# Score masks added by an identity product in the first three chunks of a sliding-window attention and rational feed-forward kernel, with a shorter weight decoding

## The chip, the core and the metric

The kernel runs on one core of a Trainium2 chip. The core has five engines that work side by side, each through its own list of instructions in order: TensorE (PE, with its weight loads shown apart as PEld), VectorE (DVE), ScalarE (ACT), GpSimd (POOL) and SyncE (SP), which here only issues transfers. An engine that waits holds up everything behind it in its list. The metric is the time of one execution on the device, in microseconds (us); lower is better.

## The reference

Attention with a window of 64 positions over 8 batches of 576 tokens, 8 heads of 64, and then a feed-forward layer whose activation is a quotient of two polynomials with given coefficients:

```python
scores = scale * np.matmul(q, k.transpose(0, 1, 3, 2))
mask = (rel >= 0) & (rel < window)
scores = np.where(mask, scores, -1000000000.0)
scores = scores - np.max(scores, axis=-1, keepdims=True)
attn = np.exp(scores)
attn = attn / (np.sum(attn, axis=-1, keepdims=True) + 1e-09)
x = np.matmul(attn, v)                  # to 4608 tokens x 512
h = x @ w_in                            # 512 x 2048
P = a[0] + a[1] * h + a[2] * h2 + a[3] * h3
Q = 1.0 + np.abs(b[0]) * np.abs(h) + np.abs(b[1]) * h2
out = (P / (Q + 1e-6)) @ w_out          # 2048 x 512
```

The two weight matrices reach the kernel as 64-bit floating-point numbers, seen as pairs of 32-bit words.

## The kernel before

**Chunks, units and steps.** The 4608 tokens are cut into 12 chunks of 384. For each chunk the attention is done in 4 units, one for every two heads. A unit computes scores (L182), masks and scales them (L188 or L192), takes the negated maximum of each row (L198), 6 exponentials with their sums (L201), divides (L203 to L205), transposes (L212, L214), multiplies by v (L223) and leaves the result as a high part and a low part, `xh` (L228) and `xl` (L229). Then each chunk takes 16 steps of the feed-forward layer, 192 in all. A step has a first product of 12 matmuls (L239, result `h` in PSUM, two buffers), a gate (L246 to L260: five ACT instructions, seven on DVE for the first 28 gates and six on DVE and one on POOL after that) that ends with the parts `gh` and `gl`, and a second product of 9 matmuls (L280) that adds to three PSUM tiles. The second product of a step is written three steps behind its first.

**Scores share one place.** Scores and transposes of all units use the same PSUM tile `ps_s`, of which there is one buffer (L175, L210). Whoever writes it next waits until the last reader of what stands there is done.

**Weights.** A weight tile (128 x 512 numbers, 512 KB) is loaded into one of two buffers `w_st` (L105, L107) and decoded into a high and a low part: ACT takes the absolute value of the high words (L113), DVE works through L114, L116, L117 and L118, ACT rounds the high part (L121), and DVE subtracts it (L122). L118 is the last to read the load's buffer, so it is what lets the load after next begin. There are 32 such tiles, 16 of `w_in` and 16 of `w_out`: 4 are asked for ahead of the first step, the others up to step 22.

**Order.** The code names, for each step, which loads, units and products belong to it; a scheduler then sets the order of every engine's list from that, so the lists interleave decoding, units and gates. While weights are decoded, DVE's list holds all three kinds of work. The division of a unit (L205) is on DVE in the first two chunks and on POOL from the third on.

Of the kernel before, what the change touches and what calls it, by code (L numbers as in the profile page):

```python
# [9 lines left out]
F32 = mybir.dt.float32  # L10
# [9 lines left out]
PR = TC // 2  # L20
# [5 lines left out]
NEG = -1.0e9  # L26
BIG = 3.0e38
# [4 lines left out]
def swa_rational_ffn(ctx: ExitStack, tc: tile.TileContext, qT, kT, v, w_in, w_out, a, b, out):  # L32
# [32 lines left out]
    mask = const.tile([P, NM, P], F32, name="mask")  # L65

    def make_mask():
        nc.gpsimd.memset(mask, BIG)
        for j in range(NM):
            for half in range(2):  # L70
                off = 0 if FIRST.get(j) == half else WIN
                r = mask[half * 64:half * 64 + 64, j, :]
# [5 lines left out]
                                        fill=NEG, base=WIN - 1 - off, channel_multiplier=-1)  # L78

# [11 lines left out]
    make_identity(nc, ident)  # L91

# [8 lines left out]
    def decode(src, hi, lo):  # L101
# [11 lines left out]
        nc.scalar.activation(cf, w.bitcast(F32)[:, :, 1], AF.Abs)  # L113
        nc.vector.tensor_scalar(out=cf, in0=cf, scalar1=2.0 ** -15, scalar2=None, op0=ALU.max)  # L114

        nc.vector.tensor_scalar(out=c, in0=c, scalar1=3, scalar2=0x3FFFFFF8, op0=ALU.logical_shift_left, op1=ALU.bitwise_and)  # L116
        nc.vector.scalar_tensor_tensor(out=c, in0=low, scalar=29, in1=c, op0=ALU.logical_shift_right, op1=ALU.bitwise_or)  # L117
        nc.vector.scalar_tensor_tensor(out=c, in0=high, scalar=0xC0000000, in1=c, op0=ALU.bitwise_and, op1=ALU.bitwise_or)  # L118
        if len(hi.shape) == 3:
            cf = cf.rearrange("p (c n) -> p c n", c=hi.shape[1])  # L120
        nc.scalar.copy(out=hi, in_=cf)  # L121
        nc.vector.tensor_tensor(out=lo, in0=cf, in1=hi.bitcast(F32), op=ALU.subtract)  # L122
# [49 lines left out]
    def unit_scores(c, hp):  # L172
        u = live[c, hp]

        ps = ps_a.tile([P, 2, 512], F32, name="ps_s", bufs=1)  # L175
        for p in range(PR):
            for z in range(2):
                for e in range(2):
# [4 lines left out]
                                     k[:, w:w + P], start=True, stop=True)  # L183
        sm = att.tile([P, 2, PR * P], F32, name="sm")
        m0 = u["m0"]
        for z in range(2):
            if m0 is None:
                nc.vector.scalar_tensor_tensor(out=sm[:, z, :].rearrange("p (r c) -> p r c", c=P),  # L188
                                               in0=ps[:, z, 0:PR * P].rearrange("p (r c) -> p r c", c=P), scalar=SCALE,
                                               in1=mask[:, 1:2, :].broadcast_to([P, PR, P]), op0=ALU.mult, op1=ALU.min)  # L190
            else:
                nc.vector.scalar_tensor_tensor(out=sm[:, z, :], in0=ps[:, z, 0:PR * P], scalar=SCALE,  # L192
                                               in1=mask[:, m0:m0 + PR, :].rearrange("p r c -> p (r c)"),
                                               op0=ALU.mult, op1=ALU.min)
# [194 lines left out]
```

## Time and profile before

| | us |
|---|---|
| median of 3 runs (1023.78 to 1029.62) | 1024.69 |
| the profiled execution's own time | 1025.14 |
| its span, first to last instruction | 1023.3 |
| PE busy | 953.1 (93%) |
| DVE busy | 850.3 (83%) |
| ACT busy | 725.8 (71%) |
| POOL busy | 233.7 (23%) |
| mean granted TensorE clock | 0.978 |

Two parts are to be told apart: a first one of some 200 us, in which weights are decoded, and the rest. A share over the whole span mixes them. In rows of the timeline the columns are start, duration, engine, line, operation, output<-input, shapes, count, and in brackets the engine's idle time before it with what ended that. Instructions of one engine overlap a little, so what one costs in a full queue is the distance from its start to the next start, not its duration.

### The profile page before, as it was taken

The page shows a single profiled execution, that of the slowest core. Times are in us where ns is not written, and L with a number is a line of the kernel's source. Part 1 is how long each engine was busy: PE and PEld are TensorE (multiplying, and loading weights), DVE is VectorE, ACT ScalarE, POOL GpSimd, SP SyncE. Part 2 cuts the span into 40 slices and gives each one's busy share as a digit, 9 for nine tenths or more (in the row PEclk, how much of TensorE's full clock was granted, in tenths as well). Part 3 has the DMA queues.
Part 4 walks back from the last instruction along what each step waited for, and adds up shares of the span by engine and source line. Part 5 has one row for each costly group of instructions (what it writes and reads, how often), then busy time and mean ns, then how long its engine had stood idle before and what let it go on. Part 6 is the DMA issues. An engine that isn't in the chain of part 4 may idle for free.

```text
span 1023.3 us, 18244 instructions
## 1 busy us (share of the span) xinstructions
PE 953.1 (93%) x6624; PEld 840.4 (82%) x6624; DVE 850.3 (83%) x1639; ACT 725.8 (71%) x1734; POOL 233.7 (23%) x231
## 2 busy tenths in 40 slices
PE   2677876899999999999999999999999999999997
PEld 2565755788898898898898898898898898888996
DVE  5999999998878878878878878878888888888785
ACT  4675765577767867867867867867867867866664
POOL 2000010002322322322322322322322322322221
PEclk9878989899999999999999999999999999999999
DMA  6634433111112112111112112111112112100000
GB/s 197 205 99 133 133 94 111 50 50 55 60 30 60 61 31 65 64 31 58 60 30 61 61 31 65 64 32 58 60 31 60 62 31 65 65 16 2 31 1 31
DMA packets 68537, 64.09 MB, mean 63 GB/s; under 512 B 4448, under 2 KB 61792, under 8 KB 68448
## 3 DMA queue, kind: packets, MB, share of 16 engines
q1 hardware_dynamic: 68448, 62.93, 19.8%
q8 instruction: 52, 0.85, 0.4%
q14 instruction: 37, 0.30, 0.1%
HBM read 53.48 MB, written 9.44 MB: 61 GB/s over the span
## 4 chain that ended last, share of the span: by engine, by line
PE 81%; DVE 11%; ACT 3%; DMA 3%; issue 1%; POOL 0%; SPq 0%; POOLq 0%; ACTq 0%; DVEq 0%
PE o L280 37%; PE h L239 35%; PE ps_x L223 3%; PE ps_s L182 3%; PE ps_s L212 3%; DMA w_st<-w_in 1%; DVE w_c L117 1%; DMA w_st<-w_out 1%; ACT sm L201 1%; DVE w_c L118 1%; DVE num L259 1%; DVE gh L257 1%; DVE u L258 1%; DVE num L249 1%; DVE num L250 1%
## 5 line engine op out<-in xcount | busy, mean ns | idle before, releaser
L239 PE MATMUL h<-xl,wi_h 128*128 128x384 f32 x768 | 264.9, 345 | 14.8 <-DVE num L250 8.6
L239 PE MATMUL h<-xh,wi_h 128*128 128x384 f32 x768 | 260.6, 339 | 0.0
L239 PE MATMUL h<-xh,wi_l 128*128 128x384 f32 x768 | 259.7, 338 | 0.0
L280 PE MATMUL o<-wo_h,gl 128*128 128x512 f32 x576 | 238.1, 413 | 22.3 <-DVE gl L260 22.3
L252 POOL TENSOR_TENSOR u<-u,ah 128x384 f32<-128x384 f32 x164 | 166.7, 1017 | 317.3 <-ACT u L248 278.7
L280 PE MATMUL o<-wo_h,gh 128*128 128x512 f32 x576 | 231.7, 402 | 0.0
L280 PE MATMUL o<-wo_l,gh 128*128 128x512 f32 x576 | 230.2, 400 | 0.0
L249 DVE TENSOR_TENSOR num<-num,h 128x384 f32<-128x384 f32 x192 | 106.1, 553 | 108.9 <-ACT num L247 108.7
L246 ACT ACTIVATE ah<-h 128x384 f32<-128x384 f32 x192 | 94.3, 491 | 108.1 <-PE h L239 83.3
L205 POOL TENSOR_TENSOR sm<-sm,rs 128x768 f32<-128x768 f32 x40 | 61.7, 1541 | 457.9 <-DVE rs L204 352.3
L201 ACT ACTIVATE sm<-sm,nmx 128x128 f32<-128x128 f32 x288 | 111.9, 390 | 76.4 <-DVE nmx L198 76.4
L239 PEld LDWEIGHTS h<-xl,wi_h 128*128 128x128 f32 x768 | 145.4, 189 | 23.3 <-DVE num L250 11.3
L280 PEld LDWEIGHTS o<-wo_h,gl 128*128 128x128 f32 x576 | 111.3, 193 | 51.3 <-DVE gl L260 24.6
L239 PEld LDWEIGHTS h<-xh,wi_h 128*128 128x128 f32 x768 | 145.5, 189 | 4.6
L239 PEld LDWEIGHTS h<-xh,wi_l 128*128 128x128 f32 x768 | 145.4, 189 | 0.0
L248 ACT ACTIVATE u<-ah,b_sb 128x384 f32<-128x384 f32 x192 | 135.4, 706 | 0.0
L280 PEld LDWEIGHTS o<-wo_h,gh 128*128 128x128 f32 x576 | 111.2, 193 | 26.1
L257 DVE SCALAR_TENSOR_TENSOR gh<-num,a_sb,ah 128x384 fp32r<-128x384 f32 x192 | 114.8, 615 | 17.6 <-ACT ah L256 16.9
L247 ACT ACTIVATE num<-h,a_sb 128x384 f32<-128x384 f32 x192 | 128.2, 668 | 0.0
L280 PEld LDWEIGHTS o<-wo_l,gh 128*128 128x128 f32 x576 | 111.8, 194 | 19.4
L250 DVE SCALAR_TENSOR_TENSOR num<-num,a_sb,h 128x384 f32<-128x384 f32 x192 | 117.9, 614 | 5.9
L259 DVE SCALAR_TENSOR_TENSOR num<-num,a_sb,u 128x384 f32<-128x384 f32 x192 | 115.8, 620 | 0.8
(45 smaller groups left out, 1090.3 us busy)
## 6 DMA issues: line engine op xcount, KB each, us to landing
out<-ob SPq DMA_DIRECT2D x33, 256.0 KB, 2.0
w_st<-w_in SPq DMA_DIRECT2D x16, 512.0 KB, 4.4
w_st<-w_out SPq DMA_DIRECT2D x16, 512.0 KB, 3.6
q<-qT SPq DMA_DIRECT2D x32, 192.0 KB, 3.3
vt<-v SPq DMA_DIRECT2D x16, 384.0 KB, 3.4
vt<-v SPq DMA_DIRECT2D x16, 320.0 KB, 3.9
kt<-kT SPq DMA_DIRECT2D x16, 224.0 KB, 3.6
kt<-kT SPq DMA_DIRECT2D x16, 192.0 KB, 3.6
```

Of the source, the lines that this page charges most:

```text
L201: nc.scalar.activation(sm[:, j, :], sm[:, j, :], AF.Exp, bias=nmx[:, j:j + 1], accum_out=sums[:, j:j + 1])
L205: (nc.vector if c < 2 else nc.gpsimd).tensor_tensor(out=sm, in0=sm, in1=rs.unsqueeze(2).broadcast_to([P, NR, P]), op=ALU.mult)
L239: nc.tensor.matmul(h, w[:, cc, i * P:(i + 1) * P], x[c, cc], start=n == 0, stop=n == 3 * NCC - 1)
L246: nc.scalar.activation(ah, h, AF.Abs)
L247: nc.scalar.activation(num, h, AF.Identity, scale=a_sb[:, 3:4], bias=a_sb[:, 2:3])
L248: nc.scalar.activation(u, ah, AF.Identity, scale=b_sb[:, 1:2], bias=b_sb[:, 0:1])
L249: nc.vector.tensor_tensor(out=num, in0=num, in1=h, op=ALU.mult)
L250: nc.vector.scalar_tensor_tensor(out=num, in0=num, scalar=a_sb[:, 1:2], in1=h, op0=ALU.add, op1=ALU.mult)
L252: (nc.vector if n_gates[0] <= DEC else nc.gpsimd).tensor_tensor(out=u, in0=u, in1=ah, op=ALU.mult)
L257: nc.vector.scalar_tensor_tensor(out=gh, in0=num, scalar=a_sb[:, 0:1], in1=ah, op0=ALU.add, op1=ALU.mult)
L259: nc.vector.scalar_tensor_tensor(out=num, in0=num, scalar=a_sb[:, 0:1], in1=u, op0=ALU.add, op1=ALU.subtract)
L280: nc.tensor.matmul(acc[c][t], g[:, ts], w[:, i, :], start=first and n == 0, stop=last and n == 2)
```

## The change

**Masks.** The mask tile held 3e38 where a score is kept and -1e9 where not, and DVE took the smaller of mask and scaled score. It now holds 0 and -1e30 and is added. It is built in a buffer that the units use later (`sm`), and an ACT copy rounds it to the type of TensorE's single-pass products. For the first three chunks (`PEM = 3`, 12 units of 48) TensorE adds it: two products of an identity with the mask (L188 of the change) open the accumulation in `ps_s`, and the score products add to that. DVE then takes the row maximum from PSUM (L202) and scales the six numbers of each row (L203), and the exponentials read PSUM with the scale built in (L213). The two mask instructions of DVE (L188 or L192 before) are gone in these units. From the fourth chunk on DVE still scales and adds the mask, two instructions a unit as before.

**Decoding.** ACT's absolute value now also scales by 2^-111, which makes the lower bound (L114) and the clearing of the top bits in the shift (L116) needless; DVE's L114 is gone, and the factor 2^-8 that puts the exponent right again is built into the ACT copy and the DVE subtraction at the end (L125, L126).

```diff
--- before.py
+++ after.py
@@ -23,8 +23,8 @@
 LAG = 3
 W_AT = 0, 1, 2, 3
 WLEAD = len(W_AT)
-NEG = -1.0e9
-BIG = 3.0e38
+NEG = -1.0e30
+PEM = 3
 QADD = 1.0 + 1e-6
 
 
@@ -62,20 +62,22 @@
     FIRST = {0: 0, 3: 1}
     MASKS = {0: 0, 3: 2}
     NM = 5
-    mask = const.tile([P, NM, P], F32, name="mask")
+    mask = const.tile([P, NM, P], F32R, name="mask")
 
     def make_mask():
-        nc.gpsimd.memset(mask, BIG)
+        raw = att.tile([P, 2 * PR, P], F32, name="sm")
+        nc.gpsimd.memset(raw[:, 0:NM, :], 0.0)
         for j in range(NM):
             for half in range(2):
                 off = 0 if FIRST.get(j) == half else WIN
-                r = mask[half * 64:half * 64 + 64, j, :]
+                r = raw[half * 64:half * 64 + 64, j, :]
 
                 nc.gpsimd.affine_select(out=r, in_=r, pattern=[[-1, P]], compare_op=ALU.is_ge,
                                         fill=NEG, base=off, channel_multiplier=1)
 
                 nc.gpsimd.affine_select(out=r, in_=r, pattern=[[1, P]], compare_op=ALU.is_ge,
                                         fill=NEG, base=WIN - 1 - off, channel_multiplier=-1)
+        nc.scalar.copy(out=mask, in_=raw[:, 0:NM, :])
 
     a_sb = const.tile([P, 4], F32, name="a_sb")
     b_raw = const.tile([P, 2], F32, name="b_raw")
@@ -89,6 +91,8 @@
     make_mask()
     ident = const.tile([P, P], F32, name="ident")
     make_identity(nc, ident)
+    ident_r = const.tile([P, P], F32R, name="ident_r")
+    nc.scalar.copy(out=ident_r, in_=ident)
 
 
     wi_h = const.tile([P, NCC, DFF], F32R, name="wi_h")
@@ -110,16 +114,16 @@
         cf = c.bitcast(F32)
 
 
-        nc.scalar.activation(cf, w.bitcast(F32)[:, :, 1], AF.Abs)
-        nc.vector.tensor_scalar(out=cf, in0=cf, scalar1=2.0 ** -15, scalar2=None, op0=ALU.max)
-
-        nc.vector.tensor_scalar(out=c, in0=c, scalar1=3, scalar2=0x3FFFFFF8, op0=ALU.logical_shift_left, op1=ALU.bitwise_and)
+
+        nc.scalar.activation(cf, w.bitcast(F32)[:, :, 1], AF.Abs, scale=2.0 ** -111)
+
+        nc.vector.tensor_scalar(out=c, in0=c, scalar1=3, scalar2=None, op0=ALU.logical_shift_left)
         nc.vector.scalar_tensor_tensor(out=c, in0=low, scalar=29, in1=c, op0=ALU.logical_shift_right, op1=ALU.bitwise_or)
-        nc.vector.scalar_tensor_tensor(out=c, in0=high, scalar=0xC0000000, in1=c, op0=ALU.bitwise_and, op1=ALU.bitwise_or)
+        nc.vector.scalar_tensor_tensor(out=c, in0=high, scalar=0x80000000, in1=c, op0=ALU.bitwise_and, op1=ALU.bitwise_or)
         if len(hi.shape) == 3:
             cf = cf.rearrange("p (c n) -> p c n", c=hi.shape[1])
-        nc.scalar.copy(out=hi, in_=cf)
-        nc.vector.tensor_tensor(out=lo, in0=cf, in1=hi.bitcast(F32), op=ALU.subtract)
+        nc.scalar.activation(hi, cf, AF.Copy, scale=2.0 ** -8)
+        nc.vector.scalar_tensor_tensor(out=lo, in0=cf, scalar=2.0 ** -8, in1=hi.bitcast(F32), op0=ALU.mult, op1=ALU.subtract)
 
     def load_w_in(i):
         sl = slice(i * P, (i + 1) * P)
@@ -173,6 +177,15 @@
         u = live[c, hp]
 
         ps = ps_a.tile([P, 2, 512], F32, name="ps_s", bufs=1)
+        m0 = u["m0"]
+        on_pe = c < PEM
+        if m0 is None:
+            mm = mask[:, 1:2, :].broadcast_to([P, PR, P])
+        else:
+            mm = mask[:, m0:m0 + PR, :]
+        if on_pe:
+            for z in range(2):
+                nc.tensor.matmul(ps[:, z, 0:PR * P].rearrange("p (r c) -> p r c", c=P), ident_r, mm, start=True, stop=False)
         for p in range(PR):
             for z in range(2):
                 for e in range(2):
@@ -180,25 +193,27 @@
                     k = u["kt"][z * 64:z * 64 + 64].rearrange("p t s -> p (t s)")
                     w = u["kw"][j] * WIN
                     nc.tensor.matmul(ps[e * 64:e * 64 + 64, z, p * P:(p + 1) * P], u["q"][z * 64:z * 64 + 64, j, :],
-                                     k[:, w:w + P], start=True, stop=True)
-        sm = att.tile([P, 2, PR * P], F32, name="sm")
-        m0 = u["m0"]
-        for z in range(2):
-            if m0 is None:
-                nc.vector.scalar_tensor_tensor(out=sm[:, z, :].rearrange("p (r c) -> p r c", c=P),
-                                               in0=ps[:, z, 0:PR * P].rearrange("p (r c) -> p r c", c=P), scalar=SCALE,
-                                               in1=mask[:, 1:2, :].broadcast_to([P, PR, P]), op0=ALU.mult, op1=ALU.min)
-            else:
-                nc.vector.scalar_tensor_tensor(out=sm[:, z, :], in0=ps[:, z, 0:PR * P], scalar=SCALE,
-                                               in1=mask[:, m0:m0 + PR, :].rearrange("p r c -> p (r c)"),
-                                               op0=ALU.mult, op1=ALU.min)
-        sm = sm.rearrange("p z (r c) -> p (z r) c", c=P)
+                                     k[:, w:w + P], start=not on_pe, stop=not on_pe or p == PR - 1)
+        sm = att.tile([P, 2 * PR, P], F32, name="sm")
         NR = 2 * PR
         nmx = att.tile([P, NR], F32, name="nmx")
-        nc.vector.tensor_reduce(out=nmx, in_=sm, axis=AX.X, op=ALU.max, negate=True)
+        if on_pe:
+            pss = ps[:, :, 0:PR * P].rearrange("p z (r c) -> p z r c", c=P)
+            nc.vector.tensor_reduce(out=nmx.rearrange("p (z r) -> p z r", z=2), in_=pss, axis=AX.X, op=ALU.max, negate=True)
+            nc.vector.tensor_scalar(out=nmx, in0=nmx, scalar1=SCALE, scalar2=None, op0=ALU.mult)
+        else:
+            for z in range(2):
+                nc.vector.scalar_tensor_tensor(out=sm[:, z * PR:(z + 1) * PR, :],
+                                               in0=ps[:, z, 0:PR * P].rearrange("p (r c) -> p r c", c=P), scalar=SCALE,
+                                               in1=mm.bitcast(F32), op0=ALU.mult, op1=ALU.add)
+            nc.vector.tensor_reduce(out=nmx, in_=sm, axis=AX.X, op=ALU.max, negate=True)
         sums = att.tile([P, NR], F32, name="sums")
         for j in range(NR):
-            nc.scalar.activation(sm[:, j, :], sm[:, j, :], AF.Exp, bias=nmx[:, j:j + 1], accum_out=sums[:, j:j + 1])
+            if on_pe:
+                nc.scalar.activation(sm[:, j, :], ps[:, j // PR, (j % PR) * P:(j % PR + 1) * P], AF.Exp, scale=SCALE,
+                                     bias=nmx[:, j:j + 1], accum_out=sums[:, j:j + 1])
+            else:
+                nc.scalar.activation(sm[:, j, :], sm[:, j, :], AF.Exp, bias=nmx[:, j:j + 1], accum_out=sums[:, j:j + 1])
         rs = att.tile([P, NR], F32, name="rs")
         nc.vector.tensor_scalar(out=sums, in0=sums, scalar1=1e-9, scalar2=None, op0=ALU.add)
         nc.vector.reciprocal(out=rs, in_=sums)
```

**What the lists look like now.** The scheduler orders anew, so the lists differ from the first row on. First DVE at the start of the program: `w_c` is a weight tile in decoding, `nmx` the row maxima of a unit, `sums` and `rs` belong to its division. Before:

```order
L114 TENSOR_SCALAR w_c<-w_c 128x512
L192 SCALAR_TENSOR_TENSOR sm<-ps_s,mask 128x384 x2
L116 TENSOR_SCALAR w_c<-w_c 128x512
L198 TENSOR_REDUCE nmx<-sm 128x6
L117 SCALAR_TENSOR_TENSOR w_c<-w_st,w_c 128x512
L118 SCALAR_TENSOR_TENSOR w_c<-w_st,w_c 128x512
```

and of the change, at the same place:

```order
L120 TENSOR_SCALAR w_c<-w_c 128x512
L121 SCALAR_TENSOR_TENSOR w_c<-w_st,w_c 128x512
L122 SCALAR_TENSOR_TENSOR w_c<-w_st,w_c 128x512
L126 SCALAR_TENSOR_TENSOR wi_l<-w_c,wi_h 128x4x128
L120 TENSOR_SCALAR w_c<-w_c 128x512
L121 SCALAR_TENSOR_TENSOR w_c<-w_st,w_c 128x512
L122 SCALAR_TENSOR_TENSOR w_c<-w_st,w_c 128x512
L120 TENSOR_SCALAR w_c<-w_c 128x512
L202 TENSOR_REDUCE nmx<-ps_s 128x6
L121 SCALAR_TENSOR_TENSOR w_c<-w_st,w_c 128x512
L126 SCALAR_TENSOR_TENSOR wi_l<-w_c,wi_h 128x4x128
L203 TENSOR_SCALAR nmx<-nmx 128x6
```

The first unit's row maximum stood behind the beginning of the first decoding; it now stands behind two whole shift-and-merge passes and the first instruction of the third tile (L120), and its scaling (L203) behind two more decoding instructions.

Then PE at the start of the program, where `ps_s` passes from unit to unit. Before:

```order
L182 MATMUL ps_s<-kt,q 64x128 x24
L212 MATMUL ps_s<-ident,sm 128x128 x6
L182 MATMUL ps_s<-kt,q 64x128 x12
L223 MATMUL ps_x<-pT,vt 64x64 x12
L212 MATMUL ps_s<-ident,sm 128x128 x6
```

and of the change:

```order
L188 MATMUL ps_s<-mask,ident_r 128x384 x2
L195 MATMUL ps_s<-kt,q 64x128 x12
L188 MATMUL ps_s<-mask,ident_r 128x384 x2
L195 MATMUL ps_s<-kt,q 64x128 x12
L227 MATMUL ps_s<-ident,sm 128x128 x6
L188 MATMUL ps_s<-mask,ident_r 128x384 x2
L195 MATMUL ps_s<-kt,q 64x128 x12
L238 MATMUL ps_x<-pT,vt 64x64 x12
L227 MATMUL ps_s<-ident,sm 128x128 x6
```

The sequence of units, transposes (L212, now L227) and products with v (L223, now L238) is the same, with two mask products ahead of each unit's scores.

Last, DVE at the end of the decoding, where `wo_l` is the low part of the last `w_out` tile. Before, the rows around it (it is the last L122 of the list) are

```order
L118 SCALAR_TENSOR_TENSOR w_c<-w_st,w_c 128x512
L257 SCALAR_TENSOR_TENSOR gh<-num,a_sb,ah 128x384
L258 SCALAR_TENSOR_TENSOR u<-u,gh 128x384
L257 SCALAR_TENSOR_TENSOR gh<-num,a_sb,ah 128x384
L122 TENSOR_TENSOR wo_l<-w_c,wo_h 128x512
```

and of the change

```order
L202 TENSOR_REDUCE nmx<-ps_s 128x6
L265 SCALAR_TENSOR_TENSOR num<-num,a_sb,h 128x384
L126 SCALAR_TENSOR_TENSOR wo_l<-w_c,wo_h 128x512
L122 SCALAR_TENSOR_TENSOR w_c<-w_st,w_c 128x512
L275 TENSOR_TENSOR gl<-num,ah 128x384
L203 TENSOR_SCALAR nmx<-nmx 128x6
L272 SCALAR_TENSOR_TENSOR gh<-num,a_sb,ah 128x384
L126 SCALAR_TENSOR_TENSOR wo_l<-w_c,wo_h 128x512
```

Counted through DVE's list, before the last tile's subtraction follows 18 finished gates (18 `gl`, 20 gates begun), and of the change 11 finished gates (12 begun). Ahead of the first `gl` the list of before holds 11 whole decodings, and that of the change 18: the decoding is moved ahead, to between the units of the first chunk.

## The prediction

> **What bounds the kernel now.** First the page's slices of the span, 25.6 us each, tenths of busy time (9 means 90% or more):
>
> ```profile
> PE   2677876899999999999999999999999999999997
> DVE  5999999998878878878878878878888888888785
> ```
>
> DVE is full in slices 2 to 9 and PE from slice 9 on, so the kernel has two parts. The windows, cut at the end of the first gate (65.6) and where PE stops idling (202.2), give for each stretch its length and the busy us (instruction counts) of PE, PEld, DVE, ACT, POOL, then granted clock, DMA share, GB/s:
>
> ```profile
> 0.00:40.00 40.00, 16.66 (x173) 13.46 (x174) 29.40 (x59) 21.47 (x68) 6.88 (x27) 0.94 0.66 199
> 40.00:65.60 25.60, 16.22 (x171) 13.71 (x169) 24.27 (x50) 18.39 (x50) 0.00 (x0) 0.82 0.54 160
> 65.60:202.20 136.60, 104.77 (x630) 86.55 (x630) 132.21 (x264) 87.19 (x204) 7.22 (x3) 0.90 0.33 103
> 202.20:1007.60 805.40, 805.35 (x5617) 719.25 (x5618) 658.79 (x1260) 593.42 (x1406) 217.94 (x200) 1.00 0.15 46
> ```
>
> From 202.2 PE is busy 805.35 of 805.40 us: whatever PE work is left there takes its full time. Before, DVE is the bound (132.21 of 136.60). Who waited for whom in the first 205 us (us, times, longest) says how:
>
> ```profile
> PE o L280 <- DVE gl L260: 20.3, 9, 4.0
> ```
>
> PE's second products wait for the gates' last DVE instruction. So the end is the time at which DVE lets PE run full, plus PE's work then left, plus a tail.
>
> **What a DVE instruction costs.** In a full queue, start to next start, from DVE's timeline:
>
> ```profile
> 96.19 0.42 DVE L116 TENSOR_SCALAR w_c<-w_c 128x512 uint32<-128x512 uint32 x1
> 96.53 0.62 DVE L259 SCALAR_TENSOR_TENSOR num<-num,a_sb,u 128x384 f32<-128x384 f32 x1
> 97.05 0.69 DVE L117 SCALAR_TENSOR_TENSOR w_c<-w_st,w_c 128x512 uint32<-128x512 uint32 x1
> 97.66 1.02 DVE L192 SCALAR_TENSOR_TENSOR sm<-ps_s,mask 128x384 f32<-128x384 f32 x2
> 98.59 0.55 DVE L260 TENSOR_TENSOR gl<-num,ah 128x384 fp32r<-128x384 f32 x1
> 99.05 0.69 DVE L117 SCALAR_TENSOR_TENSOR w_c<-w_st,w_c 128x512 uint32<-128x512 uint32 x1
> ...
> 100.72 0.95 DVE L198 TENSOR_REDUCE nmx<-sm 128x6 f32<-128x768 f32 x1
> 101.59 0.68 DVE L118 SCALAR_TENSOR_TENSOR w_c<-w_st,w_c 128x512 uint32<-128x512 uint32 x1
> ...
> 105.70 0.18 DVE L203 TENSOR_SCALAR sums<-sums 128x6 f32<-128x6 f32 x1
> 105.77 0.69 DVE L122 TENSOR_TENSOR wi_l<-w_c,wi_h 128x512 fp32r<-128x512 f32 x1
> ...
> 107.47 0.42 DVE L114 TENSOR_SCALAR w_c<-w_c 128x512 f32<-128x512 f32 x1
> 107.81 0.61 DVE L257 SCALAR_TENSOR_TENSOR gh<-num,a_sb,ah 128x384 fp32r<-128x384 f32 x1
> ```
>
> L114 and L116 cost 0.34 each; L117, L118 and L122 0.60; a unit's two mask instructions 0.93; the row maximum 0.87, and the division, as long, the same; a 128x6 instruction some 0.09. A gate's seven cost 0.47 or 0.53 each (L260, L259), together 3.47. So the change removes 32 x 0.34 = 10.9 us (L114) and 12 x 0.93 = 11.2 us (masks), adds 12 x 0.09 = 1.1 us (L203), and DVE has **21.0 us** less to do, all in the part that it bounds.
>
> Edits with one answer: the shift loses its second operation but passes the same 128x512 (kept at 0.34); L122 becomes a three-operand form like L117's, 0.60 as before; ACT's scales ride on instructions that exist. The row maximum now reads PSUM: no row has a reduction from PSUM, but two of 128x384, one reading PSUM (L249), one not (L260), agree:
>
> ```profile
> L249 DVE TENSOR_TENSOR num<-num,h 128x384 f32<-128x384 f32 x192 | 106.1, 553 | 108.9 <-ACT num L247 108.7
> L260 DVE TENSOR_TENSOR gl<-num,ah 128x384 fp32r<-128x384 f32 x192 | 103.0, 553 | 1.6
> ```
>
> So I take 0.87 again; at worst twice that, +10.4 us for twelve, at best the two-a-time pace of L116 (512 in 0.34), -4. [...]
>
> On PE the 24 mask products are like first products (12 in 2.09, below), 0.175 each and 4.2 us in all. Those of the first units lie in PE's idle time; the last two units' lie where PE is full and are counted below. The mask's ACT copy comes while ACT would wait for a load.
>
> **Where the reorder puts it.** By the order's rows the lists differ at once, so I walk the change's lists by hand, with durations from these rows (the chain's columns: start, us, what):
>
> ```profile
> 7.73 0.67 ACT w_c L113
> ...
> 10.03 0.96 DVE nmx L198
> 11.01 2.42 ACT sm L201 x12
> ...
> 26.96 4.34 DMA w_st<-w_in
> ...
> 39.87 3.50 DMA w_st<-w_out
> ```
>
> and compare with these of before:
>
> ```profile
> 17.31 1.51 PE L212 MATMUL ps_s<-ident,sm 128*128 128x128 f32 x6 [5.87 <-DVE sm L205]
> 28.00 0.55 DVE L229 TENSOR_TENSOR xl<-ps_x,xh 128x384 fp32r<-128x384 f32 x1
> 47.30 0.55 DVE L229 TENSOR_TENSOR xl<-ps_x,xh 128x384 fp32r<-128x384 f32 x1
> 51.89 1.01 DVE L249 TENSOR_TENSOR num<-num,h 128x384 f32<-128x384 f32 x2
> 65.08 1.01 DVE L260 TENSOR_TENSOR gl<-num,ah 128x384 fp32r<-128x384 f32 x2
> ```
>
> The first unit's maximum now stands behind the third tile's L120. The first decoding starts at 8.4, behind ACT's 7.73 + 0.67, and its three dependent DVE instructions free the buffer at 10.3; the third tile's load starts then, lands 4.4 later, and ACT takes 0.67: L120 at 15.4, the maximum at 15.8 (10.03 in the chain of before). L203 stands behind two more decoding instructions, so the exponentials run 18.0 to 20.4 and hold `ps_s`, which before was free once DVE had masked. Unit 2: maximum 24.8, exponentials 27.0 to 29.4; only then the first transposes, 29.5 against 17.31. The third maximum (34.8) has the eighth tile's L120 between it and its L203: load asked for at 33.1, landed 37.5, L120 at 38.2, exponentials 38.6 to 41.0. First `xl` 41.5 (28.00). Then exponentials of unit 4 from 50.1 to 52.5, transposes of units 3 and 4 at 52.6 and 54.9 (each waits for `ps_s`), the last `xl` 66.4 (47.30), first gate instruction 71.3 (51.89), first gate done **83.8** (65.6). Up to there DVE's list holds 57.9 us of work by the costs above, so it idles 25.9 us, against 65.6 - 51.9 = 13.7 before. The lead eats 12.2 of the 21.0 us, but it has done 18 decodings, not 11.
>
> From the first to the 12th `gl`, where the change's decoding ends, DVE's list holds 14 decodings (2.14 each), 11 gates, 4 maxima, 2 divisions, 4 `xl` and the small ones: 75.1 us. The 20th `gl` of before is
>
> ```profile
> 202.67 0.56 DVE L260 TENSOR_TENSOR gl<-num,ah 128x384 fp32r<-128x384 f32 x1
> ```
>
> and from the first to there the list of before held 129.4 us by the same costs and took 203.2 - 65.6 = 137.6, 1.064 of it. With that, 75.1 x 1.064 = 80 and the 12th `gl` comes at **163.8**.
>
> PE's two kinds of products, undisturbed, from the chain:
>
> ```profile
> 970.05 4.19 PE h L239 x24
> 974.24 4.14 PE o L280 x18
> ```
>
> 2.09 for a first product of 12 and 2.07 for a second of 9. From the 12th `gl` on DVE needs 28.1 us for the next 8 gates and PE 34, so PE is full from then on, 38 us sooner than at 202.2. But it has more left: by the order's count 15 first and 11 second products are done, where before it was 22 and 18. That is 7 x (2.09 + 2.07) = 29.1, one unit's scores and two units' transposes, 0.8 each (an estimate: half of the 1.51 of the transposes at 17.31, when PE ran at half its pace), and the last two units' masks 0.7: 32.3 us. Gain: 202.2 - 163.8 - 32.3 = 6.1 us.
>
> The tail of before:
>
> ```profile
> 1013.64 0.51 PE L280 MATMUL o<-wo_h,gl 128*128 128x512 f32 x1 [1.95 <-DVE gl L260]
> ```
>
> There four second products end the list: two run, PE waits 1.95 us for a gate, and two follow. Now one first product and three second ones end it, with one wait of about 2.9 for the last gate and half as much PE work behind it, which a lowered clock could stretch: within 1 us either way, taken as 0. So the span comes to 1023.3 - 6.1 = 1017.2, and the time to 1025.14 - 6.1 = **1019.0**, from the profiled execution's own time, which is 0.45 over the median of the runs and within their spread.
>
> **The rivals.**
>
> *The lead's holes close.* If loads land earlier than in the walk, or the waits fall elsewhere, DVE idles 13.7 as before: first gate 71.6, 12th 151.6, and the gain is 18.3: 1006.8. For it: loads wait only for buffers, DMA share 0.66. Against: the reorder's rows put the maxima behind loads whatever their speed. Chance 0.22.
>
> *The lead starves more.* The slow side: two buffers feed 16 decodings ahead of the first gate, and DVE's list now has little else. If a load takes 6.0 us instead of 3.5 to 4.4, some ten waits in the lead grow by 1.7: first gate at 101, 1036. It costs more than it gains from 0.6 us a load on. For it: in the first 40 us DMA already moves 199 GB/s; against: those loads landed in 4.34 and 3.50 there. Chance 0.12.
>
> *PE becomes late in the middle.* Exponentials now hold `ps_s` 2.4 us longer, and PE's list is in order: four units there, some 10 us, would push first products behind gates. PE has 56 us of work in those 80 (62 at clock 0.90), so 18 of slack must be gone first; if 6.1 us come through, nothing is won: 1025. Chance 0.12.
>
> *PE stays at a low clock.* After a wait PE runs slowly:
>
> ```profile
> 55.48 0.69 PE L239 MATMUL h<-xl,wi_h 128*128 128x384 f32 x1 [5.46 <-DVE num L250]
> 55.97 0.52 PE L239 MATMUL h<-xh,wi_h 128*128 128x384 f32 x1
> 56.29 0.52 PE L239 MATMUL h<-xh,wi_l 128*128 128x384 f32 x1
> ...
> 59.62 0.34 PE L239 MATMUL h<-xh,wi_h 128*128 128x384 f32 x1
> 59.80 0.34 PE L239 MATMUL h<-xh,wi_l 128*128 128x384 f32 x1
> ```
>
> 0.32 from start to start, and 0.18 four us later. At half the clock throughout, the middle's 56 us of PE work take 113, not 80, and it ends at 1052; it decides from a mean clock below 0.70. The lowest of the windows above is 0.82. Chance 0.04. [...]
>
> **How the numbers follow.** The walk's outcome has 0.50, with 7 us either way for load times, the PSUM reduction and the factor 1.064: 1012 to 1026. The range leaves out the lower half of the first rival (0.11), most of the starved lead and the low clock (0.11 together): 1006 to 1030. One per cent, about what a measurement of this kernel can tell from no change, is 1014.4 and 1034.9 around the median. Faster: nearly all of the first rival and a sixth of the forecast, 0.29. Slower: half of the starved lead and the low clock, 0.10. Within: 0.61.
>
> **What would show it.** In the profile of the changed kernel: no L114 on DVE, 24 mask instructions fewer, L203 at some 0.1; first exponentials about 18 and first transposes about 29.5; first gate done about 84, PE full from about 164; a row maximum from PSUM of about 0.95. The forecast is wrong if the first gate ends before 75 or after 92, if DVE idles more than 8 us between there and the last decoding, or if PE is not full after it.

## The result and the profile after

The changed kernel takes 1017.36 us (median of 5 runs, 1016.28 to 1019.73) where the kernel before takes 1025.91 beside it (5 runs, 1023.78 to 1029.62): a ratio of **0.9932, 95% interval 0.9916 to 0.9948**, about 7 us (the medians of these five runs alone are 8.6 apart). Forecast were 1019.0, a range of 1006 to 1030, and a change within 1%. The profiled execution itself took 1017.36, its span is 1015.6 (1023.3 before).

The page's slices of the changed kernel, 25.4 us each, in tenths of busy time, with the granted clock below them:

```profile
PE   1467889999999999999999999999999999999997
...
DVE  4789999887988887787788788888888788787885
...
PEclk9969999999999999999999999999999999999999
```

PE is at 90% or more from slice 7 on; before, it was from slice 9 on. DVE starts lower (4 and 7 where it had 5 and 9). The windows of the same run, cut at the end of the first gate (84.9), of the eighth (about 135.8) and where PE stops waiting (164.3), give for each stretch its length and the busy us (instruction counts) of PE, PEld, DVE, ACT, POOL, then granted clock, DMA share, GB/s:

```profile
0.00:40.00 40.00, 10.48 (x108) 7.48 (x108) 23.02 (x43) 17.53 (x50) 6.92 (x27) 1.00 0.60 181
40.00:84.90 44.90, 29.34 (x236) 24.13 (x238) 39.00 (x76) 30.15 (x84) 0.00 (x0) 0.77 0.64 191
84.90:135.80 50.90, 40.27 (x321) 32.95 (x315) 50.79 (x103) 38.45 (x97) 0.00 (x0) 0.97 0.48 148
135.80:164.30 28.50, 25.14 (x161) 21.11 (x162) 27.99 (x57) 21.66 (x50) 3.40 (x2) 1.00 0.28 84
164.30:1000.00 835.70, 834.64 (x5798) 745.13 (x5797) 686.21 (x1310) 611.84 (x1451) 222.24 (x201) 1.00 0.15 45
```

From 164.3 PE is busy 834.64 of 835.70 us; before, that began at 202.2. Up to the first gate DVE is busy only 62.0 of 84.9 us; between there and 164.3 it loses 0.6 us in all. PE's waits in the first 170 us (us, times, longest), of which the second answers to the row shown of before, where it was 20.3:

```profile
PE h L254 <- DVE num L265: 13.1, 8, 2.9
...
PE o L295 <- DVE gl L275: 2.1, 2, 1.7
```

Second products hardly wait for gates any more; first products wait now, a little at a time.

The lead, from the timeline of the changed kernel (start, duration, engine, line, what, count, and in brackets the wait and what ended it):

```profile
15.67 0.95 DVE L202 TENSOR_REDUCE nmx<-ps_s 128x6 f32<-128x768 f32 x1
...
18.00 0.37 ACT L213 ACTIVATE sm<-ps_s,nmx 128x128 f32<-128x128 f32 x1 [2.18 <-DVE nmx L203]
...
29.38 1.51 PE L227 MATMUL ps_s<-ident,sm 128*128 128x128 f32 x6 [6.63 <-ACT sm L213]
...
38.42 0.43 DVE L120 TENSOR_SCALAR w_c<-w_c 128x512 uint32<-128x512 uint32 x1 [1.82 <-ACT w_c L118]
38.76 0.17 DVE L203 TENSOR_SCALAR nmx<-nmx 128x6 f32<-128x6 f32 x1
...
41.63 0.56 DVE L244 TENSOR_TENSOR xl<-ps_x,xh 128x384 fp32r<-128x384 f32 x1
...
72.52 0.55 DVE L264 TENSOR_TENSOR num<-num,h 128x384 f32<-128x384 f32 x1
...
84.32 0.55 DVE L275 TENSOR_TENSOR gl<-num,ah 128x384 fp32r<-128x384 f32 x1
```

The transposes wait 6.63 us for exponentials that hold `ps_s`, the scaling at 38.76 stands behind a decoding that waits for its load, and the first gate ends at 84.9 instead of 65.6, as the walk had it.

### The profile page after: what moved, and what is told of

The parts are those of the page before. It is cut to its first block, busy times and chain, and to the rows that moved or that the text cites. A ratio compares the mean times of both kernels' runs of the same rounds, so it can differ in the third digit from the quotient of the medians.

```text
span 1015.6 us, 18264 instructions
## 1 busy us (share of the span) xinstructions
PE 949.6 (93%) x6648; PEld 838.1 (83%) x6648; DVE 832.9 (82%) x1595; ACT 724.1 (71%) x1736; POOL 233.6 (23%) x231
## 3 DMA queue, kind: packets, MB, share of 16 engines
q1 hardware_dynamic: 68448, 62.93, 20.2%
## 4 chain that ended last, share of the span: by engine, by line
PE 77%; DVE 14%; ACT 3%; DMA 3%; issue 2%; POOL 0%; SPq 0%; POOLq 0%; ACTq 0%; DVEq 0%
PE o L295 34%; PE h L254 34%; PE ps_x L238 3%; PE ps_s L195 3%; DMA w_st<-w_in 3%; PE ps_s L227 2%; DVE w_c L121 2%; DVE gh L272 1%; DVE w_c L122 1%; DVE num L274 1%; DVE u L273 1%; DVE gl L275 1%; DVE num L264 1%; DVE num L265 1%; DVE nmx L202 1%
## 5 line engine op out<-in xcount | busy, mean ns | idle before, releaser
L295 PE MATMUL o<-wo_h,gl 128*128 128x512 f32 x576 | 230.6, 400 | 5.2 <-DVE gl L275 5.2
L295 PE MATMUL o<-wo_h,gh 128*128 128x512 f32 x576 | 227.1, 394 | 0.0
L295 PE MATMUL o<-wo_l,gh 128*128 128x512 f32 x576 | 226.4, 393 | 0.0
L220 POOL TENSOR_TENSOR sm<-sm,rs 128x768 f32<-128x768 f32 x40 | 59.4, 1484 | 443.5 <-DVE rs L219 314.2
L272 DVE SCALAR_TENSOR_TENSOR gh<-num,a_sb,ah 128x384 fp32r<-128x384 f32 x192 | 117.2, 621 | 24.8 <-ACT ah L271 24.7
L295 PEld LDWEIGHTS o<-wo_h,gl 128*128 128x128 f32 x576 | 108.6, 189 | 31.3 <-DVE gl L275 6.7
L295 PEld LDWEIGHTS o<-wo_h,gh 128*128 128x128 f32 x576 | 108.6, 189 | 23.2
L216 ACT ACTIVATE sm<-sm,nmx 128x128 f32<-128x128 f32 x216 | 83.9, 390 | 60.1 <-DVE nmx L209 60.1
L295 PEld LDWEIGHTS o<-wo_l,gh 128*128 128x128 f32 x576 | 108.8, 189 | 18.4
L274 DVE SCALAR_TENSOR_TENSOR num<-num,a_sb,u 128x384 f32<-128x384 f32 x192 | 116.0, 618 | 0.5
```

The costliest lines, as they stand in the source:

```text
L216: nc.scalar.activation(sm[:, j, :], sm[:, j, :], AF.Exp, bias=nmx[:, j:j + 1], accum_out=sums[:, j:j + 1])
L220: (nc.vector if c < 2 else nc.gpsimd).tensor_tensor(out=sm, in0=sm, in1=rs.unsqueeze(2).broadcast_to([P, NR, P]), op=ALU.mult)
L272: nc.vector.scalar_tensor_tensor(out=gh, in0=num, scalar=a_sb[:, 0:1], in1=ah, op0=ALU.add, op1=ALU.mult)
L274: nc.vector.scalar_tensor_tensor(out=num, in0=num, scalar=a_sb[:, 0:1], in1=u, op0=ALU.add, op1=ALU.subtract)
L295: nc.tensor.matmul(acc[c][t], g[:, ts], w[:, i, :], start=first and n == 0, stop=last and n == 2)
```

## The experiments

Two facts of the code matter for them. The feed-forward steps of the first two chunks are written in four passes of eight: steps 1 to 8 of the first chunk, 1 to 8 of the second, 9 to 16 of the second, 9 to 16 of the first. And the four attention units of the second chunk are written at the steps 0, 0, 1 and 3 of the first pass. So the ninth gate of the program needs all of the second chunk's x, whose last part is its fourth `xl`, the eighth of the program.

### Which part brings it, and is it the lead?

The first group sets theory A, the prediction's own reading (the longer lead eats most of what DVE saves, so a kernel gains what its own first gate and the work behind it say), against a rival B, which gives each of the first three kernels about half of the gain, a ratio of 0.9965.

**The decoding alone**, in the kernel before:

```diff
-        nc.scalar.activation(cf, w.bitcast(F32)[:, :, 1], AF.Abs)
-        nc.vector.tensor_scalar(out=cf, in0=cf, scalar1=2.0 ** -15, scalar2=None, op0=ALU.max)
-        nc.vector.tensor_scalar(out=c, in0=c, scalar1=3, scalar2=0x3FFFFFF8, op0=ALU.logical_shift_left, op1=ALU.bitwise_and)
+        nc.scalar.activation(cf, w.bitcast(F32)[:, :, 1], AF.Abs, scale=2.0 ** -111)
+        nc.vector.tensor_scalar(out=c, in0=c, scalar1=3, scalar2=None, op0=ALU.logical_shift_left)
...
```

> The shorter decoding alone, masks as before. Theory A (the exponentials of the first chunk, reading ps_s, lengthen the lead; after the decoding PE is the bound): the lead stays short, first gl at about 70 us instead of 84.9, 13th gl at about 162, span about 1010, ratio to before 0.987: faster than the whole change. Rival B (the gain is the DVE work removed, wherever it lies): 10.9 of 21.0 us are removed, so about half of the change's gain, span about 1019.5, ratio 0.9965.

Measured: 1025.2 us, ratio 1.0008 (0.9998 to 1.0017). Both theories miss: 10.9 us less on DVE and no gain.

**The masks alone**: the changed kernel with the decoding of before.

```diff
-        nc.scalar.activation(cf, w.bitcast(F32)[:, :, 1], AF.Abs, scale=2.0 ** -111)
+        nc.scalar.activation(cf, w.bitcast(F32)[:, :, 1], AF.Abs)
+        nc.vector.tensor_scalar(out=cf, in0=cf, scalar1=2.0 ** -15, scalar2=None, op0=ALU.max)
...
```

> The masks on PE alone, decoding as before. Theory A: the lead is as long as in the change (first gl at about 86), 15th gl at about 185, span about 1023.5, ratio 1.000: the masks' 10.1 us of DVE work are eaten by the lead. Rival B: the other half of the gain, span about 1019.5, ratio 0.9965.

Measured: 1027.46 us, ratio 1.0032 (1.002 to 1.0043), first gate at 86.0. So the masks on PE are what makes the lead long, and alone they lose. Neither part gains, both together gain 0.7%: the parts don't add (1.0008 x 1.0032 = 1.0040, not 0.9932).

**The changed kernel with the first chunk's masks on DVE**, which gives DVE back 4 x (0.93 - 0.09) = 3.4 us:

```diff
-        on_pe = c < PEM
+        on_pe = 1 <= c < PEM
```

> The change, but the four units of the first chunk mask on DVE and their exponentials read SBUF (identity product for the second and third chunk only). Theory A: first gl at about 66, 13th gl at about 156, span about 1005, ratio 0.982: faster than the change by some 10 us. Rival B: 4 x 0.84 = 3.4 us more DVE work than the change, so slower than it: span about 1019, ratio 0.9965.

Measured: 1017.87 us, ratio 0.9941 (0.9928 to 0.9954). Its first gate ends at 68.6, 16 us sooner, as theory A says, and its time is that of the changed kernel. **So the long lead is not what the change loses by itself**: without it the same time comes out. Theory A falls here.

**The changed kernel with the first four weight loads written one unit later**:

```diff
-W_AT = 0, 1, 2, 3
+W_AT = 1, 2, 3, 4
```

> The change, but the four leading weight loads are asked for one unit later; the first row maximum then stands ahead of the third tile in DVE's list. Tells two causes of the long lead apart. If the loads in front of the maxima cause it: first exponentials at about 15 instead of 18.0 and the first gl at 79 or earlier. If the exponentials' hold on ps_s does: first gl within 2 us of 84.9. The time hardly changes in either case (decoding ends earlier in the order, PE has more left): span 1012 to 1017.

Measured: 1036.98 us, ratio 1.0119 (1.0106 to 1.0132). The first gate is at 86.3, hardly later, so the third tile ahead of the first row maximum isn't what makes the lead long: it now comes behind, and yet the first exponentials start at 17.98, as at 18.00, because the first two decodings now begin at 11.5 and fill DVE up to that maximum. Loads ahead of the maxima in general aren't ruled out by this. But with the same work the time is 19 us worse, far outside the 1012 to 1017 expected. Something in the middle decides.

### What happens at the ninth gate

The timelines name it. Of DVE's rows these are the eighth `gl`, the second chunk's last `xl` and the ninth `gl`. Before (the `xl` comes first):

```profile
113.15 0.55 DVE L229 TENSOR_TENSOR xl<-ps_x,xh 128x384 fp32r<-128x384 f32 x1
...
116.74 0.55 DVE L260 TENSOR_TENSOR gl<-num,ah 128x384 fp32r<-128x384 f32 x1
...
130.52 0.55 DVE L260 TENSOR_TENSOR gl<-num,ah 128x384 fp32r<-128x384 f32 x1
```

In the changed kernel the `xl` comes first by far:

```profile
124.54 0.55 DVE L244 TENSOR_TENSOR xl<-ps_x,xh 128x384 fp32r<-128x384 f32 x1
...
135.67 0.55 DVE L275 TENSOR_TENSOR gl<-num,ah 128x384 fp32r<-128x384 f32 x1
...
142.56 0.55 DVE L275 TENSOR_TENSOR gl<-num,ah 128x384 fp32r<-128x384 f32 x1
```

With the first chunk's masks on DVE it comes after the eighth gate, and DVE's rows between show waits:

```profile
116.74 0.55 DVE L275 TENSOR_TENSOR gl<-num,ah 128x384 fp32r<-128x384 f32 x1
117.81 0.43 DVE L120 TENSOR_SCALAR w_c<-w_c 128x512 uint32<-128x512 uint32 x1 [0.53 <-ACT w_c L118]
...
121.33 0.69 DVE L126 SCALAR_TENSOR_TENSOR wo_l<-w_c,wo_h 128x512 fp32r<-128x512 f32 x1 [0.68 <-ACT wo_h L125]
...
122.94 0.55 DVE L244 TENSOR_TENSOR xl<-ps_x,xh 128x384 fp32r<-128x384 f32 x1
124.88 0.43 DVE L120 TENSOR_SCALAR w_c<-w_c 128x512 uint32<-128x512 uint32 x1 [1.39 <-ACT w_c L118]
...
140.68 0.55 DVE L275 TENSOR_TENSOR gl<-num,ah 128x384 fp32r<-128x384 f32 x1
```

With the decoding alone, likewise:

```profile
117.27 0.52 DVE L260 TENSOR_TENSOR gl<-num,ah 128x384 fp32r<-128x384 f32 x1
...
126.60 0.55 DVE L229 TENSOR_TENSOR xl<-ps_x,xh 128x384 fp32r<-128x384 f32 x1
...
144.61 1.01 DVE L260 TENSOR_TENSOR gl<-num,ah 128x384 fp32r<-128x384 f32 x2
```

By the ends of these rows and of those of the other two kernels, the ninth gate ends 17.4 to 18.0 us after that `xl` in five kernels of six (22.7 us in the one with later loads), whatever the eighth does. Call the distance from the end of the eighth `gl` to the end of the ninth the hole; DVE can be busy in it. It is 13.8 us before, 6.9 in the changed kernel, 23.9 and 27.3 in these two, 24.3 with later loads. **Theory C**: this wait for the second chunk's x decides the middle. The changed kernel's long lead is hidden, because its eight gates come so late that the second chunk is ready; a kernel that reaches its eighth gate sooner only waits longer for the ninth. **Theory D**, the rival: DVE works on decodings through such a hole, so an order is worth nothing and only its amount of work counts. For the kernel before, D's premise is true: DVE is busy 24.50 of the 25 us in which its hole lies (the third of the five engines in the row).

```profile
117.00:142.00 25.00, 20.46 (x131) 16.67 (x130) 24.50 (x50) 19.49 (x54) 1.77 (x1) 0.92 0.39 118
```

### Holes closed and opened

The first four kernels of the next group make the first pass 11 gates long (then 11 of the second chunk and 5 of each), so that gates 9 to 11 need no second chunk. The edit does more than that: the code takes from `H` also when weight tiles are asked for (14 of the 28 by step 6 instead of 11, the last at step 19 instead of 22) and when the third chunk's units are written (steps 24 to 27 instead of 21, 23, 25, 27). No run separates these:

```diff
-    H = NF // 2
+    H = 11
```

In the changed kernel, where there is no hole:

> The changed kernel, with the first pass over the first chunk made of 11 gates instead of 8 (then 11 of the second chunk, then the remaining 5 of each). Theory C (the second chunk's last xl, against the eighth gate of the first chunk, decides the middle): in the changed kernel that xl starts at 124.5 us and the eighth gl ends at 136.2, so PE has work there already and nothing waits for the second chunk; the time stays at 1017 (1014 to 1020). Theory D (only how much DVE has to do up to the last decoding counts, the order is worth nothing): 1017 too. First gl unchanged at 85.

Measured: 1022.59 us, ratio 0.9981 (0.9968 to 0.9994): 5 us worse, where both theories had no change. Its ninth gate needs no second chunk any more and still ends 18.0 us after that `xl` (144.24 and 126.22), so in the changed kernel this distance need not be a wait for the x.

In the kernel with the first chunk's masks on DVE:

> The kernel with the first chunk's masks on DVE (1017.9 us, first gl done at 68.6, eighth at 117.3, second chunk's last xl only at 122.9, ninth gl at 141.2), now with a first pass of 11 gates. Theory C: gates 9 to 11 need no second chunk, so the 24 us hole between the eighth and the ninth gl shrinks to about 10, PE's idle time between 85 and 205 falls from 22 us to about 16, and the time to about 1011 (1008 to 1014). Theory D: DVE worked through that hole on decodings, nothing is won by another order: 1018 within 3.

Measured: 1012.85 us, **ratio 0.9881 (0.9857 to 0.9904)**, the fastest kernel of all, 5 us below the changed one. The hole:

```profile
117.30 0.58 DVE L275 TENSOR_TENSOR gl<-num,ah 128x384 fp32r<-128x384 f32 x1
...
125.81 0.57 DVE L244 TENSOR_TENSOR xl<-ps_x,xh 128x384 fp32r<-128x384 f32 x1
...
128.01 0.57 DVE L275 TENSOR_TENSOR gl<-num,ah 128x384 fp32r<-128x384 f32 x1
```

The `xl` is as late as before, but the ninth gate no longer asks for it, and the hole is 10.7 us.

In the kernel before with the new decoding:

> The kernel before with the new decoding alone (1025.2 us, eighth gl done at 117.8, second chunk's last xl at 126.6, ninth gl at 145.1), now with a first pass of 11 gates. Theory C: the hole of 27 us closes to about 12, PE's idle time between 85 and 205 falls from 29 us to about 22, and the time to about 1018 (1014 to 1021). Theory D: 1025 within 3.

Measured: 1014.62 us, ratio 0.9906 (0.9885 to 0.9927), with a hole of 12.3 us. That is 10.6 us below the decoding alone, and 8.9 below the kernel before beside it (1023.48).

In the kernel before:

> The kernel before, with a first pass of 11 gates. Its second chunk's last xl starts at 113.2, before its eighth gl at 117.3, and only the ninth gl at 131.0 comes late. Theory C: little to win, 1024 (1021 to 1027); if it falls as far as the two kernels with the shorter decoding do, theory C is wrong on why they were held up. Theory D: 1024.

Measured: 1029.43 us, ratio 1.005 (1.0031 to 1.007), 6 us worse. That is above the 1021 to 1027 of theory C. So the longer pass costs some 5 to 6 us in this kernel and the changed one, whose x is ready before the eighth gate, and wins 5 and 10.6 where it comes late. That is C's sign; why the pass costs 5 us by itself isn't settled, nor what its other loads and units bring: DVE idles 1.8 us more in the first 170 us of both, which is a part of it. Between the two kernels with a pass of 11, this one and the last, the decoding is worth 14.8 us (1029.43 and 1014.62), more than the 10.9 that it takes off DVE, where with passes of eight it was worth nothing.

Two kernels keep the passes of eight and move the second chunk's units alone. Earlier, in the kernel with the first chunk's masks on DVE:

```diff
-                p = max(s - prev + every * k - AHEAD, 0)
+                p = (0, 0, 1, 1)[k] if c == 1 else max(s - prev + every * k - AHEAD, 0)
```

> The kernel with the first chunk's masks on DVE (1017.9 us, short lead, eighth gl done at 117.3, second chunk's last xl at 123.5, ninth gl at 141.2), with that chunk's last unit written two steps earlier and the first pass of 8 gates as it was. So far the ninth gl ended 17.4 to 18.0 us after that xl in five kernels of six. Theory C: the xl ends at about 112, before the eighth gl, the ninth gl then at about 130, and the time falls by about 5 us to 1013 (1010 to 1016). Theory D (the order is worth nothing while DVE works): 1018 within 3.

Measured: 1016.13 us, ratio 0.9924 (0.9909 to 0.994), which doesn't differ surely from 0.9941 without the edit. The `xl` did come early and the hole is 12.6 us:

```profile
114.88 0.56 DVE L244 TENSOR_TENSOR xl<-ps_x,xh 128x384 fp32r<-128x384 f32 x1
...
122.52 0.55 DVE L275 TENSOR_TENSOR gl<-num,ah 128x384 fp32r<-128x384 f32 x1
...
135.10 0.54 DVE L275 TENSOR_TENSOR gl<-num,ah 128x384 fp32r<-128x384 f32 x1
```

A hole of half the length, and little won: here C fails on the size, and the time lies within D's 1018 within 3. The ninth gate now ends 20.2 us after the `xl`, so the 17.4 to 18.0 of the first kernels isn't a fixed delay. Later, in the changed kernel, with nothing else changed:

```diff
+                p = (0, 1, 2, 3)[k] if c == 1 else max(s - prev + every * k - AHEAD, 0)
```

> The changed kernel, with the second chunk's units written at the steps 0, 1, 2, 3 instead of 0, 0, 1, 3. Its work is the same and its first gl still ends at about 85. Theory C: the second chunk's last xl comes after the eighth gl (at about 143 instead of 125.1), the ninth gl 18 us later, near 160 instead of 143, and the time rises by about 10 us, to 1027 (1022 to 1032). Theory D: 1017 within 3.

Measured: 1035.04 us, ratio 1.0104 (1.0087 to 1.0122): 18 us worse than the changed kernel with the same work, more than the 1022 to 1032 of theory C, and the hole is there (24.3 us; the ninth gate ends 14.8 us after the `xl`):

```profile
137.12 0.52 DVE L275 TENSOR_TENSOR gl<-num,ah 128x384 fp32r<-128x384 f32 x1
...
146.51 0.56 DVE L244 TENSOR_TENSOR xl<-ps_x,xh 128x384 fp32r<-128x384 f32 x1 [0.27 <-ACT xh L243]
...
161.34 1.01 DVE L275 TENSOR_TENSOR gl<-num,ah 128x384 fp32r<-128x384 f32 x2
```

D is wrong: the order alone moves the time by 18 us. How much of it the ninth gate's wait makes is less sure, because the scheduler orders all lists anew: DVE idles 3.5 us in this hole, and 3.0 between 85 and 117 us already, where it idles 0.1 in the changed kernel.

**What a hole costs.** The windows over the first 170 us tell a part of it (same columns as above; the third engine is DVE). With the first chunk's masks on DVE:

```profile
0.00:170.00 170.00, 112.33 (x848) 92.58 (x849) 151.01 (x290) 112.59 (x286) 10.19 (x29) 0.89 0.49 151
```

the same with the second chunk's x early:

```profile
0.00:170.00 170.00, 113.40 (x873) 93.34 (x874) 151.12 (x293) 113.12 (x296) 11.72 (x30) 0.91 0.50 154
```

and with the pass of 11:

```profile
0.00:170.00 170.00, 118.38 (x902) 97.44 (x903) 154.89 (x301) 116.16 (x293) 9.99 (x29) 0.95 0.49 152
```

DVE loses 19.0, 18.9 and 15.1 us. The early x closed the hole but only moved DVE's idle time forward; the pass of 11 took 3.9 us of it away, and PE was busy 6 us more (118.38 for 112.33) and at a higher clock (0.95 for 0.89). So among these three the time follows what DVE idles, and not the hole's length. (Decodings alone don't fill DVE: in the 23.9 us of the first kernel's hole it waits 2.9 us for two steps on ACT, as the bracketed rows show in part, and ACT waits 3.1 us there for the loads.) For all kernels, from the same windows (work removed by the costs of the prediction; gain is 1023.3 less the span, both of one profiled execution, which lies up to 2.4 us off the median of its runs):

| kernel | DVE work removed | DVE idle in the first 170 us | removed less added idle | gain |
|---|---|---|---|---|
| before | 0 | 15.8 | 0 | 0 |
| changed | 21.0 | 23.6 | 13.2 | 7.7 |
| decoding alone | 10.9 | 20.2 | 6.5 | 0.7 |
| masks alone | 10.1 | 23.5 | 2.4 | -4.3 |
| first chunk's masks on DVE | 17.6 | 19.0 | 14.4 | 7.6 |
| ... and x early | 17.6 | 18.9 | 14.5 | 8.5 |
| ... and pass of 11 | 17.6 | 15.1 | 18.2 | 14.6 |
| decoding alone, pass of 11 | 10.9 | 15.4 | 11.2 | 11.9 |
| before, pass of 11 | 0 | 17.5 | -1.8 | -4.0 |
| changed, pass of 11 | 21.0 | 25.4 | 11.4 | 1.9 |
| changed, loads later | 21.0 | 30.9 | 5.8 | -12.0 |
| changed, x late | 21.0 | 33.2 | 3.6 | -8.1 |

The fourth column puts the kernels in roughly the order of the fifth; the kernel before, the masks alone and the two with loads or x late are out of place. The gain is smaller by 2 to 10 us in most. The decoding alone with the pass of 11 seems to have no such rest, but by its ratio its gain is 9.6. The last two rows have 18 and 12 us more, which the column doesn't explain.

What PE has got done explains them. From about 162 us on PE is full in the kernel with x late as well (48.06 of the 48.10 us to 210), as it is from 164.3 in the changed one, but it comes there with less done. The changed kernel, and below it the one with x late (the first busy time is PE's, the clock is the third number from the end):

```profile
85.00:170.00 85.00, 71.01 (x526) 58.90 (x522) 84.28 (x170) 64.47 (x154) 3.40 (x2) 0.98 0.38 117
```

```profile
85.00:170.00 85.00, 63.20 (x385) 52.73 (x386) 76.18 (x149) 54.91 (x135) 1.47 (x1) 0.84 0.36 111
```

Counted to 205 us, where PE is full in both, the changed kernel has done 24.0 first and 20.9 second products, the one with x late 20.0 and 18.0, the one with loads later 20.2 and 18.0. At 2.09 and 2.07 us each that is 14.3 and 14.0 us, and with one unit's scores (0.9), two mask products (0.4) and one or two units' transposes (0.8 each) that are missing too some 16.5 and 17, of spans that are 15.8 and 19.7 longer. The same count, with 0.9 for a unit's product with v, comes within 3 us of the gain for each of the twelve kernels. So what an order costs is the PE work that is missing when PE runs full, the prediction's own terms; what DVE idles is one cause of it, and decodings ahead of gates another: in both late kernels DVE finishes the last decoding at 157 to 159, as in the changed one, but with 8 gates done instead of 11.

### Is PE full afterwards?

```diff
-PEM = 3
+PEM = 12
```

> The changed kernel with the masks added on PE in all twelve chunks. Both theories hold that PE is the bound once DVE has finished decoding. The 36 further units take 72 mask products of 0.175 us more on PE, 12.6 us, and 72 mask instructions of 0.465 us less on DVE, 33 us. If PE is full there, the time rises by 12.6 less what the exponentials from PSUM save, to about 1029 (1026 to 1032); if DVE held anything up there, it rises less or falls.

Measured: 1035.05 us, ratio 1.0118 (1.0098 to 1.0138), above the expected range; the span is 17.0 us above the changed kernel's. PE waits 0.9 us in all from 165 on, so PE is the bound there. The 72 mask instructions, busy 36.4 us in the changed kernel, are gone from DVE, but the page has it busy 832.6 us, for 832.9: 36 more scalings add 6.7, and two rows of the gate (L272, L274) last 674 and 672 ns each instead of 621 and 618. Why they do stays open. But a mask product cost more than the 0.175 us taken: 17.0 / 72 = 0.24. PE's timeline in that kernel, the two mask products of a unit and its scores:

```profile
608.50 0.51 PE L188 MATMUL ps_s<-mask,ident_r 128*128 128x384 f32 x2
608.94 0.89 PE L195 MATMUL ps_s<-kt,q 64*64 64x128 f32 x24
```

The pair takes 0.44 us from start to start, not 0.35.

## Why the prediction was right, and where its reason was not

**Two parts, and the end as DVE's release plus PE's work left plus a tail**: right. PE is full from 164.3, forecast from 163.8 on.

**DVE's work removed**: the counts are right (44 DVE instructions fewer on the page, 1595 for 1639: 32 and 24 less, 12 more), and the page has DVE busy 832.9 for 850.3. The small scaling lasts 0.16 to 0.17, like the other 128x6 TENSOR_SCALAR of a unit (L218, 166 ns). By the windows DVE idles 22.9 us in the lead (25.9 in the walk) and 11.9 before (13.7). The reduction from PSUM, the unknown of the sum, was priced well; the costliest groups have both kinds side by side (count, then busy and mean ns), the one from SBUF being before's:

```profile
L202 DVE TENSOR_REDUCE nmx<-ps_s 128x6 f32<-128x768 f32 x12 | 11.4, 951 | 0.2 <-PE ps_s L195 0.2
```

```profile
L198 DVE TENSOR_REDUCE nmx<-sm 128x6 f32<-128x768 f32 x48 | 45.4, 946 | 0.0
```

951 ns from PSUM against 946 is 5 ns, or 0.06 us for all twelve, where the prediction allowed from -4 to +10.4 us.

**The walk of the lead**: right within 2 us throughout. First exponentials 18.0 (forecast 18.0), first transposes 29.4 (29.5), third exponentials 39.0 (38.6), first `xl` 41.6 (41.5), last `xl` 68.4 (66.4), first gate instruction 72.5 (71.3), first gate done 84.9 (83.8).

**The middle**: this is the term that was mis-sized. 75.1 us of work, taken times 1.064, were to last 80; they lasted 75.7 (84.9 to 160.6, the end of the 12th `gl`), a factor of 1.01. The 1.064 came from the kernel before and held that order's own losses: by the windows DVE idled 4.4 of 136.6 us there, and 0.1 of 75.7 in the changed kernel. (They don't lie in the hole of 13.8 us between the eighth and ninth gates of before, where DVE idles 0.5; 2.5 of them fall between there and 202.2.) The rest of the 8.2 us by which before took longer than its 129.4 of costs is no idle time. The 4.3 us won here, less the 1.1 by which the first gate came late, put the 12th `gl` at 160.6 for 163.8, 3.2 us to the good.

**PE's work left and the tail**: 821.1 us lay between 202.2 and the end of the span before. With the 32.3 us that the prediction adds it should have been 853.4 behind the 12th gate; it was 855.0 (160.6 to 1015.6), 1.6 more. Two things bear on that and aren't told apart. The tail, taken as 0 within 1, waits longer: once PE runs full, its waits for second products are 3.1 us after

```profile
PE o L295 <- DVE gl L275: 3.1, 2, 2.3
```

and 2.0 before

```profile
PE o L280 <- DVE gl L260: 2.0, 1, 2.0
```

And at 160.6 PE had done 14.2 first products, not the 15 of the order's count. Together -3.2 + 1.6 = -1.6, which is how far the span is below the 1017.2 forecast. That the second slip takes back half of the first is luck.

**The rivals.** *The lead's holes close* was priced at 1006.8, with nothing else late behind it. The kernel with the first chunk's masks on DVE closed the lead (first gate at 68.6, for 71.6), has 3.4 us of DVE work more, and took 1017.9, not about 1010. So the forecast came out, but the sentence in it that the lead eats 12.2 of the 21.0 us was wrong as a cause: what is late next in that kernel is the ninth gate, 23.9 us behind the eighth, behind the second chunk's x, which the prediction didn't name. A short lead paid only with the pass of 11 (1012.85), which frees that gate but moves loads and units too; the x made early by itself brought 1.7 us, which isn't clear of noise. *PE becomes late in the middle* did not come in the changed kernel, where PE's waits there are 2.9 us and less, but is much like what its variants met: between 85 and 170 us PE is busy 71.0 us in the changed kernel, 62.7 with the short lead and 55.6 with the decoding alone. *The lead starves more* and *PE stays at a low clock* didn't come: the clock was 0.77 in the second half of the lead and 0.97 to 1.00 behind it (the half clock of that rival is what the kernel before showed at its 0.32 rows: 0.50 granted from 54 to 58 us).

## What to carry to other kernels

Work taken off the bounding engine is worth only what the next thing in line lets through (here the 10.9 us less of decoding on DVE brought nothing with passes of eight, and 8.9 us against the kernel before with a pass of 11): before pricing a gain, list for the stretch behind it which input each step needs and when that input is ready, here the second chunk's x at the ninth step, and count how much of the last bound's work (here PE's products) is done when the first bound lets go. A stall that shows in the trace is not thereby a loss (here the first gate came 16 us sooner, and the time was 1017.87 for 1017.36); take it away alone, and if the time stays, look for what comes late next. And don't carry a stretch factor from one order to another: it holds that order's own holes (1.064 before, 1.01 after).

## What the runs showed of the hardware

Exponentials of 128x128 that read PSUM take 372 ns on ACT, those from SBUF 390 (72 and 216 in the changed kernel):

```profile
L216 ACT ACTIVATE sm<-sm,nmx 128x128 f32<-128x128 f32 x216 | 83.9, 390 | 60.1 <-DVE nmx L209 60.1
...
L213 ACT ACTIVATE sm<-ps_s,nmx 128x128 f32<-128x128 f32 x72 | 25.4, 372 | 4.7 <-DVE nmx L203 4.6
```

In the kernel with the masks on PE in all chunks, two neighbouring 128x384 products with an identity cost 0.44 us in the row at 608.50, or 0.24 each by the span with 72 of them more, where a long row of 128x384 first products runs at 0.175. And an order of the same work moved the time of this kernel from 1017 to 1035 us, nearly as much as all the DVE work that the change removes (21.0 us).
